# Gated linear attention with a StarReLU layer: from the eighth block on, scaled q and k are transposed by one DMA a block instead of by TensorE

## The chip, the cores and the metric

The kernel runs on one core of a Trainium2 chip. The metric is device time in microseconds (us), from the first to the last instruction of the program on that core; lower is better. The kernel before took 195.38 us (median of 3 runs, 194.61 to 196.4). The engines are called by the profile's names: PE is TensorE's matmuls and PEld its weight loads, DVE is VectorE, ACT is ScalarE, POOL is GpSimd, and SP is SyncE, which in this kernel does nothing but issue DMAs. SPq in a profile row is SP's instruction queue.

## The reference

A recurrence over 768 positions for 4 batches and 8 heads of width 48, and then a two-layer network over the 3072 resulting rows.

```
for t in range(S):
    state = alpha[:, :, t, :, None] * state + einsum('bhd,bhe->bhde', k[:, :, t], v[:, :, t])
    y[:, :, t] = einsum('bhd,bhde->bhe', q[:, :, t], state)
x = y.transpose(0, 2, 1, 3).reshape(B * S, H * D)          # 3072 x 384
h = x @ w_in                                               # 384 -> 2048
r = maximum(h, 0)
out = (s * (r * r) + b) @ w_out                            # 2048 -> 384
```

All inputs and the output are float32; the kernel multiplies in bf16 and adds up in float32.

## The kernel before

The sequence is cut into chunks of 128 positions: 6 chunks a batch, so 24 blocks, numbered n. A block goes through these steps, which are functions of the kernel:

- `load(n)`: four DMAs from SP's queue (L127) bring alpha, k, q and v of the block, 192 KB each, into rings of 8 buffers.
- `ln(n)` takes the logarithm of alpha on ACT (L192), `cum(n)` sums it along the chunk by one matmul into `ct_ps` (L199), and two activations give `bi_sb` = exp(-sum) (L210) and `b_sb` = exp(sum) (L211).
- From block 5 on, where the block is not the last of its batch, `cum` calls `decay(n)`. This takes the last row of `b_sb`, which is the decay over the whole chunk, to a small buffer in memory (`row_dr`, L219) and back into `blast`, with one value a partition (two DMAs, L221). The second step has to wait until the first has landed. All three are issued from SP.
- `vcast(n)` turns v into bf16 on POOL (L195).
- `qk(n)`: two DVE products write scaled k into `kb_sb` (L227) and then scaled q into `qb_sb` (L228), both bf16, with the heads padded from 48 to 64 columns.
- `tr(n)`: eight PE transposes against an identity (L233) write qb and kb, transposed, into PSUM (`t_ps`, the same bank as `ct_ps`), and one DVE copy (L238) takes the 112 x 1024 values into `qkT`.
- `amat(n)`: eight matmuls give k q^T for each head (L248), and two DVE products apply the causal mask (L256, `am_a` and `am_b`).
- `y(n)`: matmuls with the state so far (L267) and with the masked products (L276) give y; L287 gives the chunk's own part of the state, which DVE (L323) and POOL (L328, L332) add and multiply by `blast`.
- `xt(n)` transposes y (L301); `m` does four groups of 12 matmuls of the first layer (L354), with the relu on ACT (L368) and the square on DVE (L375); `o` does 16 matmuls of the second layer (L392), and the result is stored by DMA. The results of the first 14 blocks are kept on the chip and get their bias (L431) and are stored (L428) later, between the other stores, from about position 126 on.

No scheduler moves anything: each step is entered in a list with a position, and the instructions of all engines and queues are issued in the order of the positions. A block is 8 positions long, and block n's `y` stands at p = 8n. The steps ahead of it stand at p - c and so on, where from block 8 on c = 14.8 (`cum`), t = 10.8 (`tr`) and a = 7.9 (`amat`); for blocks 5 to 7 they stand closer to p. `load(n + 4)` stands at p - 2.5. Each engine and each queue works through its own instructions strictly in that order, and an instruction that waits holds everything behind it.

All bulk DMAs, the small ones of `decay` and the stores are issued from SP's queue. The tiles of the pipeline are rings: 2 buffers of `qb_sb`, 3 of `kb_sb`, 2 of `qkT`, 3 of `b_sb` and `blast`.

Of the kernel before, what the change touches and what calls it, by code (L numbers as in the profile page):

```python
# [9 lines left out]
BF16 = mybir.dt.bfloat16  # L10
AF = mybir.ActivationFunctionType
ALU = mybir.AluOpType

@with_exitstack
def kernel(
# [12 lines left out]
    nc = tc.nc  # L28

    B, H, S, D = q.shape  # L30
    C = 128
    NCH = S // C
# [9 lines left out]
    UNITS = 5  # L42
    assert sum(GROUPS) == NBLK
    NLD = 8

    ctx.enter_context(tc.manual_schedule())
    sb = ctx.enter_context(tc.tile_pool(name="sb", bufs=1))
# [16 lines left out]
    def ring(name, shape, dtype, n):  # L64
        return [sb.tile(shape, dtype, name=f"{name}{i}") for i in range(n)]
# [9 lines left out]

    q_sb = ring("q_sb", [128, H, 48], FP32, NLD)
    k_sb = ring("k_sb", [128, H, 48], FP32, NLD)
    v_sb = ring("v_sb", [128, H, 48], FP32, NLD)
    al_sb = ring("al_sb", [128, H, 48], FP32, NLD)
    la_sb = ring("la_sb", [128, H, 64], BF16, 2)  # L80
    b_sb = ring("b_sb", [128, H, 48], FP32, 3)
    bi_sb = ring("bi_sb", [128, H, 48], FP32, 2)
    qb_sb = ring("qb_sb", [128, H, 64], BF16, 2)
    kb_sb = ring("kb_sb", [128, H, 64], BF16, 3)
    v_bf = ring("v_bf", [128, H, 48], BF16, 3)
    y_bf = ring("y_bf", [128, H * 48], BF16, 2)
    qkT_sb = ring("qkT", [128, 2, NP, 128], BF16, 2)
    am_sb = [ring("am_a", [128, NP, 128], BF16, 2), ring("am_b", [128, NP, 128], BF16, 2)]
    blast = ring("blast", [128, NP, 1], FP32, 3)
    row_dr = [dr.tile([1, H * 48], FP32, name=f"row_dr{i}") for i in range(3)]  # L90
# [27 lines left out]
    def src(t, n):  # L118
        b, c = n // NCH, n % NCH
        return t[b, :, c * C : (c + 1) * C, :].rearrange("h s d -> s h d")  # L120

    def load(n, parts=1):
        if n < NBLK:
            for dst, t in ((al_sb, alpha), (k_sb, k), (q_sb, q), (v_sb, v)):
                for i in range(parts):
                    hs = slice(i * H // parts, (i + 1) * H // parts)
                    nc.sync.dma_start(out=dst[n % NLD][:, hs], in_=src(t, n)[:, hs])  # L127

# [62 lines left out]
    def ln(n):  # L191
        nc.scalar.activation(out=la_sb[n % 2][:, :, 0:48], in_=al_sb[n % NLD], func=AF.Ln)  # L192

# [3 lines left out]
    def cum(n):  # L197
        la = la_sb[n % 2]
        nc.tensor.matmul(out=cum_ps, lhsT=U_bf, rhs=la[:, :, 0:48], start=True, stop=True)  # L199
        if n < NCH - 1:  # L200
            for p in range(NP):
                nc.tensor.matmul(  # L202
                    out=tot_ps[0:112, p : p + 1],
                    lhsT=la.rearrange("a h d -> a (h d)")[:, 128 * p : 128 * p + 112],
                    rhs=ones_c,
                    start=True,
                    stop=True,
                )
        cv = cum_ps.rearrange("a (h d) -> a h d", h=H)
        nc.scalar.activation(out=bi_sb[n % 2], in_=cv, func=AF.Exp, scale=-1.0)  # L210
        nc.scalar.activation(out=b_sb[n % 3], in_=cv, func=AF.Exp)  # L211
        if n < NCH - 1:
            nc.scalar.activation(out=blast[n % 3][0:112, :, 0], in_=tot_ps[0:112], func=AF.Exp)
        elif n % NCH < NCH - 1:
            decay(n)

    def decay(n):
        row = row_dr[n % 3]
        nc.sync.dma_start(out=row, in_=b_sb[n % 3].rearrange("s h d -> s (h d)")[127:128])  # L219
        for e in range(2):  # L220
            nc.sync.dma_start(  # L221
                out=blast[n % 3][64 * e : 64 * e + 48, :, 0],
                in_=row.rearrange("o (p e d) -> e d (o p)", e=2, d=48)[e],
            )

    def qk(n):
        nc.vector.tensor_tensor(out=kb_sb[n % 3][:, :, 0:48], in0=k_sb[n % NLD], in1=bi_sb[n % 2], op=ALU.mult)  # L227
        nc.vector.tensor_tensor(out=qb_sb[n % 2][:, :, 0:48], in0=q_sb[n % NLD], in1=b_sb[n % 3], op=ALU.mult)  # L228

    def tr(n):  # L230
        for x, t in ((0, qb_sb[n % 2]), (1, kb_sb[n % 3])):
            for p in range(NP):
                nc.tensor.transpose(  # L233
                    out=t_ps[0:112, x, p, :],
                    in_=t.rearrange("a h d -> a (h d)")[:, 128 * p : 128 * p + 112],
                    identity=ident,
                )
        nc.vector.tensor_copy(  # L238
            out=qkT_sb[n % 2][0:112].rearrange("a x p t -> a (x p t)"),
            in_=t_ps[0:112].rearrange("a x p t -> a (x p t)"),  # L240
        )
# [209 lines left out]
    for t in la_sb:  # L451
        nc.vector.memset(t, 0.0)
    nc.vector.memset(ones_c, 1.0)
    for t in qb_sb + kb_sb + blast:
        nc.vector.memset(t, 0.0)
    make_identity(nc, ident)
    for i in range(NP):
# [8 lines left out]
    def at(pos, fn, *args):  # L466
        events.append((pos, len(events), fn, args))
# [24 lines left out]
    for pos, what in enumerate(  # L492
        [
            (ln, 0), (vcast, 0), (cum, 0), (qk, 0), (spread,), (busy, 3), (tr, 0), (busy, 1), (ln, 1), (vcast, 1), (amat, 0),
            (cum, 1), (busy, 3), (yp, 0), (qk, 1), (st, 0), (busy, 1), (tr, 1), (xt, 0), (busy, 2), (amat, 1),
            (win, 0), (win, 1), (busy, 5), (yp, 1), (ln, 2), (st, 1), (busy, 1), (xt, 1), (cum, 2), (mr, 0, 0), (vcast, 2),
            (qk, 2), (mr, 0, 1), (sq, 0, 0), (mr, 0, 2), (mr, 0, 3), (tr, 2), (sq, 0, 1), (busy, 3), (amat, 2), (sq, 0, 2),
            (win, 2), (busy, 5), (ln, 3), (yp, 2), (st, 2), (cum, 3), (mp, 0, 4), (xt, 2), (rl, 0, 4), (vcast, 3), (qk, 3),
            (mr, 0, 5), (sq, 0, 3), (mr, 1, 0), (sq, 0, 4), (tr, 3), (mr, 1, 1), (sq, 0, 5), (amat, 3), (win, 3), (mr, 1, 2),
            (sq, 1, 0), (busy, 2, y_ps), (yp, 3), (sq, 1, 1), (st, 3), (mr, 0, 6), (xt, 3), (mr, 0, 7), (sq, 1, 2), (sq, 0, 6),  # L500
            (wout, 0), (mr, 1, 3), (sq, 0, 7), (m, 2, 0), (sq, 1, 3), (m, 2, 1), (wout, 1), (o, 0, 0), (m, 2, 2), (o, 1, 0),
            (m, 2, 3), (o, 2, 0), (wout, 2), (o, 0, 1), (o, 1, 1), (colsum, 1), (ln, 4), (wout, 3), (o, 2, 1), (cum, 4), (o, 0, 2), (vcast, 4), (qk, 4), (o, 1, 2), (o, 2, 2), (colsum, 2), (o, 0, 3),
            (o, 1, 3), (tr, 4), (o, 2, 3), (o, 3, 0), (amat, 4),
        ]
    ):
        at(0.1 * pos, *what)
# [12 lines left out]
    for n in range(4, NBLK):  # L519
        p = 8 * n  # L520
        if n > 4:
            f = min((n - 5) / 3.0, 1.0)
            c, t, a = 9.0 + 5.8 * f, 5.8 + 5.0 * f, 3.4 + 4.5 * f
            at(p - c - 1.9, ln, n)
            at(p - c + 0.01, vcast, n)
            at(p - c, cum, n)
            at(p - c + 0.2, qk, n)
            at(p - t, tr, n)
            at(p - a, amat, n)

        e = 0.8 if n == NBLK - 1 else 0.0
        at(p - e, y, n)
        if n + 4 < NBLK:
            at(p - 2.5, load, n + NLD - 4)
        for u in range(4):
            at(p + (2.5, 3.5, 5.5, 7.5)[u], m, group_of[n][0], u)
            at(p + (8.5, 9.5, 12.5, 14.5)[u], o, n, u)
        at(p + 1.0 - e, xt, n)
# [32 lines left out]
```

## Time and profile before

| | |
|---|---|
| median of the runs | 195.38 us (194.61, 195.38, 196.4) |
| span of the profiled execution | 194.6 us |
| granted TensorE clock | 1.000 |
| PE busy | 183.1 us (94%), 2390 matmuls |
| DVE busy | 152.4 us (78%) |
| ACT busy | 119.3 us (61%) |
| POOL busy | 62.1 us (32%) |
| DMA queue of SP | 113550 packets, 29.94 MB, 76.4% of 16 engines' span |

The page gives no time of its own for the profiled execution beside the span of 194.6 us; it lies next to the fastest of the three runs, 0.8 us under their median. Busy time is a share of the whole span, and the stages differ: the first 42 us are the start with the loads of the weights, then follow the blocks at an even pace, and the last 5 us are the tail of the second layer. In every stretch of 14 us between 60 and 186 us PE is busy for 13.88 us or more.

Two kinds of rows are used below. Rows of the timeline give the start, the length, the engine, the line and operation, the tile written and the tiles read, and in brackets how long the engine was idle before and what ended it. Rows of the chain give the start, the length and the work on the chain that ended last. The end of a matmul is modelled, so its cost is read from start to start.

### The profile page before, as it was taken

How to read it: one execution, taken by the hardware profiler on the slowest of the kernel's cores; microseconds unless marked ns; L12 is line 12 of the kernel's file. 1: busy time of each engine (PE TensorE's matmuls, PEld its weight loads, DVE VectorE, ACT ScalarE, POOL GpSimd, SP SyncE). 2: the span in 40 equal slices, each digit the busy share in tenths (PEclk: the TensorE clock that was granted, in tenths of full speed). 3: DMA queues.
4: the chain of work that ended last, by engine and by line, in shares of the span. 5: the costliest groups of instructions: out<-in, count | busy, mean ns of one | idle time of the engine just before them, and what ended most of it. 6: DMA issues, size and time to landing. Idle time of an engine off the chain costs nothing.

```text
span 194.6 us, 6011 instructions
## 1 busy us (share of the span) xinstructions
PE 183.1 (94%) x2390; PEld 144.4 (74%) x2390; DVE 152.4 (78%) x295; ACT 119.3 (61%) x244; POOL 62.1 (32%) x96
## 2 busy tenths in 40 slices
PE   0998978999999999999999999999999999999994
PEld 0566566856777788778878888888877977877783
DVE  5477779965687788888887996878988999998532
ACT  3346395673677666766677576675675666654640
POOL 5143250401300515624500642642501563352000
PEclk9999999999999999999999999999999999999999
DMA  7999889999995856984958458959795965433212
GB/s 124 190 333 176 228 157 369 367 176 198 187 171 90 161 95 93 151 140 79 183 94 163 88 92 152 154 88 192 140 217 148 210 135 115 128 119 121 84 40 81
DMA packets 113581, 30.31 MB, mean 156 GB/s; under 512 B 106755, under 2 KB 112018, under 8 KB 113554
## 3 DMA queue, kind: packets, MB, share of 16 engines
q1 hardware_dynamic: 113550, 29.94, 76.4%
q8 instruction: 18, 0.29, 0.7%
q14 instruction: 9, 0.07, 0.1%
q10 hardware_dynamic: 4, 0.00, 0.0%
HBM read 25.19 MB, written 4.74 MB: 154 GB/s over the span
## 4 chain that ended last, share of the span: by engine, by line
PE 74%; SPq 14%; DMA 6%; ACT 2%; issue 1%; DVE 1%; ACTq 0%
PE o_ps L392 28%; PE h_ps L354 27%; SPq L127 11%; DMA al_sb<-in_alpha_dram 6%; PE ct_ps L233 5%; PE a_ps L248 3%; PE h_ps L301 2%; PE y_ps L276 2%; SPq L136 2%; PE ct_ps L199 2%; PE a_ps L415 1%; PE a_ps L392 1%; PE y_ps L267 1%; SPq L131 1%; PE p_ps L287 1%
## 5 line engine op out<-in xcount | busy, mean ns | idle before, releaser
L368 ACT ACTIVATE r_sb<-h_ps 128x512 bf16<-128x512 f32 x92 | 54.7, 596 | 35.5 <-PE h_ps L354 33.4
L354 PE MATMUL h_ps<-xd_all,w_in_bf 128*128 128x128 bf16 (+1 forms) x1074 | 72.9, 220 | 0.4 <-ACT w_in_bf L143 0.3
L354 PEld LDWEIGHTS <-w_in_bf 128*128 128x128 bf16 x1104 | 68.0, 98 | 7.0 <-issue 0.5
L392 PE MATMUL o_ps<-w_out_bf,gt_all 128*128 128x384 bf16 x336 | 68.3, 326 | 0.1
L375 DVE TENSOR_TENSOR gt_all<-r_sb 128x512 bf16<-128x512 bf16 x96 | 46.8, 503 | 22.2 <-ACT r_sb L368 21.6
L328 POOL TENSOR_TENSOR sd_sb<-t_sb,blast 48x192 bf16<-48x192 f32 x40 | 20.2, 506 | 90.0 <-DVE t_sb L323 54.7
L392 PEld LDWEIGHTS <-gt_all 128*128 128x128 bf16 x368 | 32.6, 98 | 16.1
L195 POOL CAST v_bf<-v_sb 128x384 bf16<-128x384 f32 x24 | 17.0, 710 | 25.1 <-DMA v_sb<-in_v_dram 24.9
L332 POOL TENSOR_TENSOR sc_sb<-t_sb,blast 112x384 f32<-112x384 f32 x16 | 22.6, 1413 | 1.3
L307 ACT ACTIVATE xd_all<-h_ps 128x384 bf16<-128x384 bf16 x24 | 11.8, 490 | 14.3 <-PE h_ps L301 14.3
L238 DVE COPY qkT<-ct_ps 112x1024 bf16<-112x1024 bf16 x24 | 16.4, 682 | 4.9 <-PE ct_ps L233 3.4
L227 DVE TENSOR_TENSOR kb_sb<-k_sb,bi_sb 128x384 bf16<-128x384 f32 x24 | 13.6, 568 | 6.9 <-ACT bi_sb L210 6.8
L256 DVE TENSOR_TENSOR am_a<-a_ps,mask 128x512 bf16<-128x512 f32 x24 | 16.4, 684 | 2.5 <-PE a_ps L248 2.5
L228 DVE TENSOR_TENSOR qb_sb<-q_sb,b_sb 128x384 bf16<-128x384 f32 x24 | 16.4, 683 | 0.9 <-ACT r_sb L368 0.9
L256 DVE TENSOR_TENSOR am_b<-a_ps,mask 128x512 bf16<-128x512 f32 x24 | 16.3, 681 | 0.0
L192 ACT ACTIVATE la_sb<-al_sb 128x384 bf16<-128x384 f32 x24 | 12.4, 517 | 4.1 <-DMA al_sb<-in_alpha_dram 3.9
L210 ACT ACTIVATE bi_sb<-ct_ps 128x384 f32<-128x384 f32 x24 | 11.7, 487 | 4.5 <-PE ct_ps L202 3.5
L199 PE MATMUL ct_ps<-la_sb,U_bf 128*128 128x384 bf16 x24 | 8.1, 340 | 6.1 <-ACT la_sb L192 6.1
L294 ACT ACTIVATE y_bf<-y_ps 128x384 bf16<-128x384 f32 x24 | 11.7, 487 | 1.6 <-PE y_ps L276 1.6
L211 ACT ACTIVATE b_sb<-ct_ps 128x384 f32<-128x384 f32 x24 | 11.8, 493 | 0.0
L233 PEld LDWEIGHTS <-qb_sb 128*112 128x112 bf16 x96 | 8.7, 136 | 3.8 <-DVE qb_sb L228 2.5
L248 PE MATMUL a_ps<-qkT 48*128 48x128 bf16 x192 | 9.8, 222 | 0.8 <-DVE qkT L238 0.7
(67 smaller groups left out, 197.4 us busy)
## 6 DMA issues: line engine op xcount, KB each, us to landing
al_sb<-in_alpha_dram SPq DMA_DIRECT2D x22, 192.0 KB, 3.5
k_sb<-in_k_dram SPq DMA_DIRECT2D x22, 192.0 KB, 4.0
q_sb<-in_q_dram SPq DMA_DIRECT2D x22, 192.0 KB, 4.3
v_sb<-in_v_dram SPq DMA_DIRECT2D x22, 192.0 KB, 4.3
w_in_st<-in_moe_w_in_dram SPq DMA_DIRECT2D x4, 768.0 KB
w_out_st<-in_moe_w_out_dram SPq DMA_DIRECT2D x4, 768.0 KB, 9.7
out_dram<-w_in_st SPq DMA_DIRECT2D x14, 192.0 KB, 2.0
out_dram<-out_sb SPq DMA_DIRECT2D x9, 192.0 KB
```

Of the source, the lines that this page charges most:

```text
L127: nc.sync.dma_start(out=dst[n % NLD][:, hs], in_=src(t, n)[:, hs])
L195: nc.gpsimd.tensor_copy(out=v_bf[n % 3], in_=v_sb[n % NLD])
L228: nc.vector.tensor_tensor(out=qb_sb[n % 2][:, :, 0:48], in0=q_sb[n % NLD], in1=b_sb[n % 3], op=ALU.mult)
L233: nc.tensor.transpose(out=t_ps[0:112, x, p, :], in_=t.rearrange("a h d -> a (h d)")[:, 128 * p : 128 * p + 112], identity=ident,)
L238: nc.vector.tensor_copy(out=qkT_sb[n % 2][0:112].rearrange("a x p t -> a (x p t)"), in_=t_ps[0:112].rearrange("a x p t -> a (x p t)"),)
L256: nc.vector.tensor_tensor(out=am_sb[e][n % 2], in0=a_ps[e], in1=mask4, op=ALU.mult)
L328: nc.gpsimd.tensor_tensor(out=sd[r, :, d], in0=t1_sb[r, :, d], in1=bl[r].to_broadcast([48, NP, 48]), op=ALU.mult)
L332: nc.gpsimd.tensor_tensor(out=sc_sb[0:112], in0=t1_sb[0:112], in1=bl[0:112].to_broadcast([112, NP, 96]), op=ALU.mult)
L354: nc.tensor.matmul(out=hp[:, jj * N : (jj + 1) * N], lhsT=w_in_bf[:, kk, 128 * j : 128 * (j + 1)], rhs=xd_sb[g][:, kk, 0:N], start=(kk == ...
L368: nc.scalar.activation(out=rs, in_=h_of.pop((g, u)), func=AF.Relu)
L375: nc.vector.tensor_tensor(out=gt_sb[g][:, u * 512 : (u + 1) * 512], in0=rs, in1=rs, op=ALU.mult)
L392: nc.tensor.matmul(out=op[:, 0:d_model], lhsT=gt_sb[g][:, j * N + t * C : j * N + (t + 1) * C], rhs=w_out_bf[:, j, :], start=(j == 0), sto ...
```

## The change

Scaled q and k of a block now lie in one tile, `qk_sb` (128 x 2 x 8 x 64, a ring of 3), and `qb_sb` and `kb_sb` are views of it, so `qb_sb` has three buffers and no longer two. From block 7 on (`XBAR = 7`) `tr(n)` issues no PE instruction and no DVE copy: one transposing DMA, from SP's queue, reads the 128 x 1024 bf16 values of `qk_sb` (256 KB) and writes `qkT`. These are 17 of the 24 blocks.

Three steps move. `tr(n)` of these blocks stands 1.4 positions behind `cum(n)`, at p - 13.4, where it stood at p - 10.8. `decay` is split: the row goes out from `cum` as before, and the two DMAs that bring it back stand 0.1 position behind `tr`, for every block that has them. `load(n + 4)` of these blocks stands at p - 5.0 and not p - 2.5. `amat` and all that follows keep their positions.

```diff
-    qb_sb = ring("qb_sb", [128, H, 64], BF16, 2)
-    kb_sb = ring("kb_sb", [128, H, 64], BF16, 3)
+    qk_sb = ring("qk_sb", [128, 2, H, 64], BF16, 3)
+    qb_sb = [t[:, 0] for t in qk_sb]
+    kb_sb = [t[:, 1] for t in qk_sb]
...
         elif n % NCH < NCH - 1:
-            decay(n)
+            nc.sync.dma_start(out=row_dr[n % 3], in_=b_sb[n % 3].rearrange("s h d -> s (h d)")[127:128])
 
     def decay(n):
+        if n < NCH - 1 or n % NCH == NCH - 1:
+            return
         row = row_dr[n % 3]
-        nc.sync.dma_start(out=row, in_=b_sb[n % 3].rearrange("s h d -> s (h d)")[127:128])
         for e in range(2):
             nc.sync.dma_start(
...
     def tr(n):
-        for x, t in ((0, qb_sb[n % 2]), (1, kb_sb[n % 3])):
+        if n >= XBAR:
+            nc.sync.dma_start_transpose(
+                out=qkT_sb[n % 2].rearrange("a x p t -> a (x p) t"),
+                in_=qk_sb[n % 3].rearrange("a x h d -> a (x h d)"),
+            )
+            return
+        for x, t in ((0, qb_sb[n % 3]), (1, kb_sb[n % 3])):
...
             at(p - c + 0.2, qk, n)
+            if n >= XBAR:
+                t = c - 1.4
             at(p - t, tr, n)
+            at(p - t + 0.1, decay, n)
             at(p - a, amat, n)
...
         if n + 4 < NBLK:
-            at(p - 2.5, load, n + NLD - 4)
+            at(p - (5.0 if n >= XBAR else 2.5), load, n + NLD - 4)
```

In the instruction lists of the two kernels, PE loses 17 x 8 transposes with their weight loads, DVE loses 17 copies, and SP's queue gains 17 transposing DMAs. From block 8 on its order within a block is: row, transposing DMA, two DMAs of `blast`, four loads, and then the stores where there are any. Each transposing DMA waits for DVE (the products of `qk`) and for PE (the last reader of that `qkT` buffer, two blocks earlier); the first weight load of `amat` waits for the DMA.

More of the change, by code (lines that the diff above doesn't have):

```diff
@@ L44 @@
     NLD = 8
+    XBAR = 7
     ctx.enter_context(tc.manual_schedule())
@@ L227, in qk @@
         nc.vector.tensor_tensor(out=kb_sb[n % 3][:, :, 0:48], in0=k_sb[n % NLD], in1=bi_sb[n % 2], op=ALU.mult)
-        nc.vector.tensor_tensor(out=qb_sb[n % 2][:, :, 0:48], in0=q_sb[n % NLD], in1=b_sb[n % 3], op=ALU.mult)
+        nc.vector.tensor_tensor(out=qb_sb[n % 3][:, :, 0:48], in0=q_sb[n % NLD], in1=b_sb[n % 3], op=ALU.mult)
     def tr(n):
-        for x, t in ((0, qb_sb[n % 2]), (1, kb_sb[n % 3])):
+        if n >= XBAR:
[5 more added lines that the diff above has]
+        for x, t in ((0, qb_sb[n % 3]), (1, kb_sb[n % 3])):
             for p in range(NP):
@@ L453 @@
     nc.vector.memset(ones_c, 1.0)
-    for t in qb_sb + kb_sb + blast:
+    for t in qk_sb + blast:
         nc.vector.memset(t, 0.0)
```

## The prediction

> **What bounds the kernel now.** I read the chain of waits first. It runs through PE for 74% of the span; before 42 us it is the start's DMAs, which the change leaves alone. One block of it:
>
> ```profile
> 102.70 0.65 PE o_ps L392 x4
> 103.36 0.45 PE ct_ps L233 x8
> 103.80 0.67 PE h_ps L354 x12
> ...
> 106.17 0.33 PE a_ps L248 x8
> 106.50 0.76 PE o_ps L392 x4
> 107.25 0.17 PE h_ps L301 x3
> 107.42 0.16 PE ct_ps L199
> ```
>
> The pieces follow one another without a gap: PE is the bound, and the eight transposes (L233) cost it 0.45 us a block. `amat` (L248) stands 2.8 us behind them, and the next block's `cum` (L199) 1.2 us behind that. Blocks 8 to 23 take PE (171.15 - 65.83)/15 = 7.02 us each, from one start of L199 or L248 to the next.
>
> Second, DVE's timeline in the same stretch, for the slack ahead of `amat`:
>
> ```profile
> 101.97 0.55 DVE L228 TENSOR_TENSOR qb_sb<-q_sb,b_sb 128x384 bf16<-128x384 f32 x1
> ...
> 104.05 0.68 DVE L238 COPY qkT<-ct_ps 112x1024 bf16<-112x1024 bf16 x1
> ```
>
> With `cum` of this block at 100.39, qb is ready at 102.52 (2.13 us later) and `amat` starts at 106.10. So a transposing DMA has 3.6 us, and 3.1 to 3.2 once PE loses its 0.45 us.
>
> Third, SP's timeline, since the new DMA goes into that queue:
>
> ```profile
> 103.43 1.29 SPq L127 DMA_DIRECT2D v_sb<-in_v_dram  x1
> 104.82 0.39 SPq L219 DMA_DIRECT2D row_dr<-b_sb  x1
> 107.21 0.81 SPq L221 DMA_DIRECT2D blast<-row_dr  x2
> 108.07 0.44 SPq L127 DMA_DIRECT2D al_sb<-in_alpha_dram  x1
> 108.60 0.53 SPq L127 DMA_DIRECT2D k_sb<-in_k_dram  x1
> 109.23 1.75 SPq L127 DMA_DIRECT2D q_sb<-in_q_dram  x1
> 111.03 0.94 SPq L127 DMA_DIRECT2D v_sb<-in_v_dram  x1
> 112.06 0.39 SPq L219 DMA_DIRECT2D row_dr<-b_sb  x1
> ```
>
> SP works back to back, with one wait, 2.0 us for the row to land. Row 104.82 belongs to block 13, whose `b_sb` was ready at 101.85: SP is 3 us late. It was 5.5 us late in block 7 (row at 66.33, `b_sb` at 60.8) and 6.1 in block 8, caught up by block 18, and fell 2.6 behind again by block 21. Nothing feels this now, since `blast` is needed only some 12 us after `cum`. In the changed kernel `amat` feels it at once.
>
> **Part by part.** *Removed from PE:* 17 blocks x 0.45 us = 7.65 us, on the path, so -7.65; PE's block becomes 6.57 us. The shared PSUM bank is freed too; PE waits for it nowhere in a full block, so nothing.
>
> *Removed from DVE:* 17 x 0.68 = 11.6 us. DVE is busy 5.2 to 6.9 us of each 7 and is no bound: nothing, save that it keeps up with a shorter block (fullest stretch 6.94 of 7, less 0.68, is 6.3).
>
> *The transposing DMA's latency.* No row of the trace shows one. Its floor is a `blast` DMA, 0.8 KB landing in 1.8 us; its nearest neighbour by source is a 192 KB store, 2.0 us; its ceiling is a load, 192 KB in 3.5 to 4.3 us, which by bytes is 5.7 for 256 KB. I build it from the row DMA right ahead of it: SP sees that land 2.4 to 3.1 us after its issue (104.82 to 107.21, 124.38 to 127.55), because up to two loads are still in the queue. Loads issued back to back pass at one per 1.0 us (41.90 to 53.66), so 256 KB adds 1.4. From 0.45 us after the row this makes 3.3 to 4.1; I take 3.4, near the low end, because a queue that waits for qb has drained further. PE's loop is then: latency L, 1.16 us from `amat` to the next `cum`, 2.13 to qb; so a block takes L + 3.3 = 6.7 us instead of 6.57. Over the nine blocks 8 to 16: +1.1.
>
> The Trainium skill (DMA: Bandwidth & Descriptors, Latency and other measured facts) gives 261 GB/s for a transposing DMA, and its Anatomy section a fixed 2.0 us; my estimate from it is 1.0 + 2.0 = 3.0 us, and the sum by it would lose the +1.1.
>
> *Its time on SP.* Rows go from 0.25 us (a row) to 1.9 (a throttled load). Anything up to some 2 us is hidden in the wait for the row; I take nothing, but where a block has no row (11, 17, 23) it is one more issue of 0.4 to 0.5 us, within SP's reserve there (row 10 to row 12: 11.49 us for two blocks).
>
> *Entering the regime.* Block 6's row goes out at 58.63 as now. Then stand the four loads at 1.0 us each (to 63.0), `blast` (63.9), row 7, and the transposing DMA at 64.4. With L = 3.4 it lands at 67.8; PE would reach `amat(7)` at 65.83 - 0.45 = 65.4. PE waits 2.4, once, and is coupled to SP from there. +2.4.
>
> *The stretch with stores.* SP's rows go out at 137.56, 145.19, 152.97 and 161.10: blocks of 7.63, 7.78 and 8.13 us, since two or three stores join the loads. Only slack hides this now. In the changed kernel row and transpose wait for SP, so PE's three blocks become 23.5 us instead of 19.7: +3.8, less the 0.8 us that SP waited ahead of row 18: +3.0. The lower end is nothing, if SP gets ahead.
>
> *Moved:* `blast` comes behind the transpose, the loads ahead of the stores. POOL needs block 13's `blast` (issued 107.21) at 114.42, so 5 us of cover; loads are four blocks ahead. The transpose's waits hold `blast`, loads and stores behind it on SP; with SP late, qb is ready before SP arrives. Memsets and the third buffer: nothing.
>
> Sum: -7.65 + 1.1 + 2.4 + 3.0 = -1.15 us. The profiled execution would span 193.4, and the median, 0.8 above its span, would be 194.2.
>
> **Rivals.** *A, SP and DMA keep up.* If L stays under 3.25 us and the stores hide, only the entry costs: -7.65 + 1.5 to 2.4, so 189.2 to 190.1. For it: the 192 KB store's 2.0 us; in nine blocks without stores SP needs 6.45 us on average, under PE's 6.57. Against it: SP's lateness throughout.
>
> *B, slower: the transpose is late in every block.* Place: the wait of `amat`'s first weight load. It decides from L = 3.7 us: then L + 3.3 equals today's 7.02, and nothing is won. At the loads' 4.3 us a block takes 7.6: 16 x 0.6 = +9.6, with the entry at 3.3, so 208.3; at L = 4.0, +4.5 and 3.0: 202.9; at the ceiling of 5.7 us, 16 x 2.0 + 4.7: 232. An SP that needs over 2 us to issue it acts the same way, twice: it delays L, and lengthens SP's own block. For it: my build-up of L reaches 4.1. Against it: the row's 3.1 us is at a queue that is full behind a late SP, which a PE that waits lets drain.
>
> On this the Trainium skill speaks against the change: Advanced Engine Details and Errata, DGE: Hardware vs Software, calls the transpose efficiency of hardware descriptor generation, which SP uses, the worse of the two. No row here shows it; it would be rival B.
>
> That the change doesn't take place is no rival: the instruction lists show 136 PE transposes gone.
>
> **The numbers.** A difference under about 1% (1.95 us) can't be told from none. The forecast has 0.5; its own range, with L from 3.25 to 3.6 and the stores from 0 to 3.8, is 190.5 to 197.0, of which 0.24 lies under 193.4, 0.22 within 1% and 0.04 above. Rival A has 0.16, rival B 0.34. So faster 0.40, same 0.22, slower 0.38. The range goes from 189.2 (A's best) into B as far as 207, where about 0.12 of B stays out above; with a little under 189.2, 0.15 is outside.
>
> **What would show it.** Right: PE's chain loses L233 after 62 us; `amat`'s weight load waits for DMA in most blocks, 0.1 to 0.3 us, about 2.4 us in block 7 and about 1 us in blocks 19 to 21; SP's rows 6.6 to 6.8 us apart without stores. Wrong: waits at L248 of more than 0.5 us in every block, or an SP row for the transpose above 2 us (B); none after block 8 (A). If the profile shows `amat` waiting for DVE, or POOL for `blast`, another step has failed.

## The result, and the profile after

| | before | after |
|---|---|---|
| median of 4 runs each | 195.03 us | 213.3 us (211.5 to 215.14) |
| ratio | | 1.0906 (95%: 1.0831 to 1.0981) |
| profiled execution: span, granted clock | 194.6 us, 1.000 | 213.4 us, 0.968 |

The changed kernel is 9% slower. Ratios, here and below, leave out runs more than 1.5% above the fastest of their kernel, the profiled one of 215.14 us among them. In every run on record the time is 1.7 to 1.9 us above the span; so the span of 194.6 us before belongs to the run of 196.4 us, the longest of its kernel and not one near the fastest, and the two profiles compare the longest runs of both. Line numbers move up by up to nine: `amat` is L257 (was L248), `cum` L201, the second layer L401, the first L363, `qk` L230 and L231, the row L217, `blast` L224, the loads L129; the transposing DMA is L235.

From the page of the changed kernel: PE's busy share, the granted clock in 40 slices, SP's DMA queue, and the chain by engine.

```profile
PE 182.1 (85%) x2254; PEld 140.5 (66%) x2254; DVE 140.4 (66%) x276; ACT 119.2 (56%) x244; POOL 52.2 (24%) x96
...
PEclk9999999999999799999999999999996997699999
...
q1 hardware_dynamic: 131502, 34.40, 87.1%
...
PE 56%; DMA 27%; SPq 11%; ACT 2%; issue 2%; DVE 1%; ACTq 0%
```

PE has lost 136 transposes and is busy 85% of a longer span (94% before). DMA has 27% of the chain and had 6%; the DMA into `qkT` alone has 24%. The clock, 1.0 in every slice before, now falls in three places. SP's queue moves 17,952 packets more, 1056 for each transpose. PE's two rows in the table of waits name the place:

```profile
PEld L257 <- DMA qkT<-qk_sb: 22.0, 13, 3.6
PE a_ps L257 <- DMA qkT<-qk_sb: 19.9, 13, 3.3
```

The chain in the stretch that was shown of before (start, length, work):

```profile
101.52 3.11 DMA qkT<-qk_sb
104.63 0.05 issue
104.67 0.40 PE a_ps L257 x8
...
105.99 0.16 PE ct_ps L201
...
106.81 1.22 PE h_ps L363 x22
108.03 4.28 DMA qkT<-qk_sb
112.31 0.05 issue
112.35 0.40 PE a_ps L257 x8
```

Where one PE piece followed the other without a gap, each block now closes the same loop: the transpose lands, `amat`, `cum`, the two products, the next transpose. Two things set a block: the time from the issue of the DMA to `amat` (here 3.15 and 4.32 us, called L as in the prediction), and the time from `amat` to the next issue (here 3.36). SP's timeline in the same stretch:

```profile
107.31 0.25 SPq L217 DMA_DIRECT2D row_dr<-b_sb  x1
108.03 1.24 SPq L235 DMA_TRANSPOSE qkT<-qk_sb  x1
111.56 0.81 SPq L224 DMA_DIRECT2D blast<-row_dr  x2
112.42 0.44 SPq L129 DMA_DIRECT2D al_sb<-in_alpha_dram  x1
112.91 0.57 SPq L129 DMA_DIRECT2D k_sb<-in_k_dram  x1
113.53 0.80 SPq L129 DMA_DIRECT2D q_sb<-in_q_dram  x1
114.37 0.70 SPq L129 DMA_DIRECT2D v_sb<-in_v_dram  x1
115.12 0.90 SPq L217 DMA_DIRECT2D row_dr<-b_sb  x1
116.13 1.24 SPq L235 DMA_TRANSPOSE qkT<-qk_sb  x1
```

Issuing a transpose takes SP 1.24 us, and the wait for the row behind it has grown: 4.25 us from the row's issue to `blast` here, 3.3 on the mean of the 15 rows (2.5 before). The four loads come behind that, and the next transpose (116.13) follows them by one row.

Read from the starts of L248 before, and of L235 and L257 after:

| | `amat` to `amat`, before | forecast | after | of it L | of it `amat` to next issue |
|---|---|---|---|---|---|
| start of `amat` in block 7 | 65.83 | 67.8 | 68.24 | 3.23 | |
| blocks 8 to 17, mean of 9 | 7.08 us | 6.7 | 7.68 | 4.09 | 3.59 |
| blocks 18 to 23, mean of 5 | 7.06 us | 7.8 in three of them | 9.07 | 3.85 | 5.22 |

Over all 17 transposes L falls into two groups: eight from 3.09 to 3.37 us, eight from 4.06 to 5.11, one of 3.59 between. (Where PE comes to `amat` after the landing, L is an upper bound; the 4.06, in block 22, is one of these.)

What sets the groups apart stands in the view of the DMA queues. Beside SP's queue the page has a queue q8 of the kind `instruction`, with 17 transfers of 16 KB (0.28 MB in all), and the kernel before has 18 of them. In the 3.0 us behind the issue of a transpose, such a transfer starts in seven of the 17 blocks: 9, 10, 13, 16, 17, 20 and 21, which are those with an L of 4.12 to 5.11. In the other ten none does, and L is 3.09 to 3.59 there, and 4.06 in block 22.

Three of the waits cost more than their length. Both fences are of the changed kernel: PE's timeline, with the wait in brackets, and windows; in a window row the granted clock stands third from the end, before the DMA share and GB/s.

```profile
160.11 0.40 PE L257 MATMUL a_ps<-qkT 48*128 48x128 bf16 x8 [3.15 <-DMA qkT<-qk_sb]
...
179.36 0.61 PE L257 MATMUL a_ps<-qkT 48*128 48x128 bf16 x8 [3.35 <-DMA qkT<-qk_sb]
```

```profile
157.75:161.16 3.41, 1.05 (x14) 0.69 (x14) 1.02 (x3) 0.00 (x0) 2.28 (x4) 1.00 0.62 100
161.16:164.57 3.41, 3.41 (x25) 2.56 (x24) 1.70 (x4) 1.35 (x4) 0.00 (x0) 0.50 1.11 211
...
180.00:187.00 7.00, 7.00 (x54) 5.11 (x54) 3.63 (x7) 2.56 (x6) 0.00 (x0) 0.64 0.28 65
```

With the waits of 3.20 us (block 7), 3.15 and 3.35 the clock falls to 0.50, for 3.41, 3.41 and 6.83 us (from 69.00, 161.16 and 178.23). In the window from 180 us PE is busy all 7.00 us and does 54 matmuls, where the window from 100 us has 95 in 6.67 us. The mean of 0.968 over the span is worth (1 - 0.968) x 213.4 = 6.8 us.

The account then closes: 7.65 us of transposes gone, 19.9 us of waits at `amat` added, 6.8 us of clock, together +19.05 us; measured are 213.4 - 194.6 = +18.8. By stretch, from `amat` to `amat`, +3.9 us of it lie in blocks 6 to 8, +5.4 in 8 to 17 and +10.1 in 18 to 23; the rest is under half a microsecond each.

### The profile page after: what moved, and what is told of

It is laid out like the page before. It is cut to its first block, busy times and chain, and to the rows that moved or that the text cites. A ratio compares the mean times of both kernels' runs of the same rounds, so it can differ in the third digit from the quotient of the medians.

```text
span 213.4 us, 5728 instructions
## 1 busy us (share of the span) xinstructions
PE 182.1 (85%) x2254; PEld 140.5 (66%) x2254; DVE 140.4 (66%) x276; ACT 119.2 (56%) x244; POOL 52.2 (24%) x96
## 4 chain that ended last, share of the span: by engine, by line
PE 56%; DMA 27%; SPq 11%; ACT 2%; issue 2%; DVE 1%; ACTq 0%
DMA qkT<-qk_sb 24%; PE o_ps L401 22%; PE h_ps L363 21%; SPq L129 10%; PE a_ps L257 4%; DMA w_in_st<-in_moe_w_in_dram 3%; PE a_ps L401 2%; PE h_ps L310 2%; PE ct_ps L201 2%; PE a_ps L424 1%; SPq L133 1%; PE y_ps L285 1%; ACT r_sb L377 1%; PE ct_ps L242 1%; PE y_ps L276 0%
## 5 line engine op out<-in xcount | busy, mean ns | idle before, releaser
L363 PEld LDWEIGHTS <-w_in_bf 128*128 128x128 bf16 x1104 | 71.5, 100 | 9.5 <-issue 1.5
L363 PE MATMUL h_ps<-xd_all,w_in_bf 128*128 128x128 bf16 (+1 forms) x1074 | 75.7, 225 | 0.3 <-ACT w_in_bf L145 0.3
L401 PE MATMUL o_ps<-w_out_bf,gt_all 128*128 128x384 bf16 x336 | 71.0, 336 | 0.0
L384 DVE TENSOR_TENSOR gt_all<-r_sb 128x512 bf16<-128x512 bf16 x96 | 41.9, 446 | 36.0 <-ACT r_sb L377 35.6
L401 PEld LDWEIGHTS <-gt_all 128*128 128x128 bf16 x368 | 33.3, 100 | 17.2 <-issue 1.9
L316 ACT ACTIVATE xd_all<-h_ps 128x384 bf16<-128x384 bf16 x24 | 11.8, 490 | 33.3 <-PE h_ps L310 33.3
L257 PE MATMUL a_ps<-qkT 48*128 48x128 bf16 x192 | 10.0, 226 | 20.6 <-DMA qkT<-qk_sb 19.9
L265 DVE TENSOR_TENSOR am_a<-a_ps,mask 128x512 bf16<-128x512 f32 x24 | 16.5, 689 | 14.8 <-PE a_ps L257 14.8
L230 DVE TENSOR_TENSOR qk_sb<-k_sb,bi_sb 128x384 bf16<-128x384 f32 x24 | 15.0, 627 | 11.9 <-ACT bi_sb L212 11.8
L257 PEld LDWEIGHTS <-qkT 48*128 48x128 bf16 x192 | 5.6, 97 | 25.7 <-DMA qkT<-qk_sb 22.0
L197 POOL CAST v_bf<-v_sb 128x384 bf16<-128x384 f32 x24 | 14.5, 607 | 24.6 <-DMA v_sb<-in_v_dram 24.5
L231 DVE TENSOR_TENSOR qk_sb<-q_sb,b_sb 128x384 bf16<-128x384 f32 x24 | 16.1, 673 | 0.0
L341 POOL TENSOR_TENSOR sc_sb<-t_sb,blast 112x384 f32<-112x384 f32 x16 | 15.3, 958 | 1.3
L201 PE MATMUL ct_ps<-la_sb,U_bf 128*128 128x384 bf16 x24 | 8.6, 356 | 5.5 <-ACT la_sb L194 5.5
L213 ACT ACTIVATE b_sb<-ct_ps 128x384 f32<-128x384 f32 x24 | 11.8, 493 | 0.0
L310 PE MATMUL h_ps<-ident,y_bf 128*128 128x128 bf16 x72 | 8.5, 230 | 0.9 <-ACT y_bf L303 0.8
```

The source lines that it names most:

```text
L197: nc.gpsimd.tensor_copy(out=v_bf[n % 3], in_=v_sb[n % NLD])
L231: nc.vector.tensor_tensor(out=qb_sb[n % 3][:, :, 0:48], in0=q_sb[n % NLD], in1=b_sb[n % 3], op=ALU.mult)
L257: nc.tensor.matmul(out=a_ps[e][:, p, :], lhsT=qkT[r0 : r0 + 48, 1, p, :], rhs=qkT[r0 : r0 + 48, 0, p, :], start=True, stop=True,)
L265: nc.vector.tensor_tensor(out=am_sb[e][n % 2], in0=a_ps[e], in1=mask4, op=ALU.mult)
L341: nc.gpsimd.tensor_tensor(out=sc_sb[0:112], in0=t1_sb[0:112], in1=bl[0:112].to_broadcast([112, NP, 96]), op=ALU.mult)
L363: nc.tensor.matmul(out=hp[:, jj * N : (jj + 1) * N], lhsT=w_in_bf[:, kk, 128 * j : 128 * (j + 1)], rhs=xd_sb[g][:, kk, 0:N], start=(kk == ...
```

## The experiments

The theory behind all of them is that PE waits for a transpose that lands late; what they tell apart is why it is late: traffic, the loads ahead of it, `blast`, the stores, the place of `amat`, or the queue. Each run is compared with the kernel before on the same chip. Of the twelve expectations the theory held in one (moves only) and the named rival in four (amat later; both, no loads; issue earlier from 12; ACT's queue); the other seven times lie between the two. "Transposes beside" and "no loads" were executed twice, the others four to ten times.

| | median us | before | ratio (95%) | span us, clock |
|---|---|---|---|---|
| moves only | 195.47 | 195.51 | 0.9985 (0.9958 to 1.0012) | 194.4, 1.0 |
| transposes beside | 200.02 | 195.51 | 1.0217 (1.0138 to 1.0296) | 197.5, 1.0 |
| no loads | 200.43 | 195.51 | 1.0238 (1.0171 to 1.0304) | 198.8, 1.0 |
| amat later | 208.36 | 195.51 | 1.0612 (1.0539 to 1.0685) | 204.8, 0.983 |
| blast behind the loads | 206.53 | 195.09 | 1.0535 (1.0456 to 1.0615) | 202.8, 0.983 |
| both | 201.05 | 195.09 | 1.0253 (1.0171 to 1.0336) | 197.3, 1.0 |
| both, stores late | 197.42 | 195.09 | 1.0105 (1.0068 to 1.0142) | 195.1, 1.0 |
| both, up to block 16 | 196.43 | 195.09 | 1.0053 (1.0009 to 1.0096) | 194.4, 0.991 |
| both, no loads | 197.04 | 195.24 | 1.0074 (1.0031 to 1.0116) | 194.1, 1.0 |
| issue 2.7 earlier | 196.65 | 195.24 | 1.0040 (0.9995 to 1.0084) | 195.1, 0.991 |
| issue 2.7 earlier, from 12 | 197.1 | 195.24 | 1.0101 (1.0015 to 1.0188) | 193.7, 0.998 |
| ACT's queue | 221.29 | 194.88 | 1.1248 (1.1121 to 1.1375) | 219.8, 0.961 |

### Moves only

PE turns every block; only the other moves of the change are left: the split of `decay`, the earlier loads, the common tile.

```diff
-            if n >= XBAR:
-                t = c - 1.4
             at(p - t, tr, n)
-            at(p - t + 0.1, decay, n)
+            at(p - ((c - 1.4) if n >= XBAR else t) + 0.1, decay, n)
...
-        if n >= XBAR:
+        if n >= NBLK:
             nc.sync.dma_start_transpose(
```

> The moves alone: decay split and its second half placed as in the changed kernel, the loads at p - 5.0, qk in one tile; q and k of all blocks are turned by PE and the DVE copy as before. Theory (the transposing DMA's own traffic and its wait cost the time): within 1% of before, 193.5 to 197. Rival SP (the new order of SP's queue holds something up): 200 or more.

195.47 us against 195.51. The moves cost nothing and bring nothing; the whole loss hangs on the DMA.

### Transposes beside

PE turns every block as in the run above, and the 17 transposing DMAs go out as well, into a spare tile that nothing reads.

```diff
+    def tr_beside(n):
+        nc.sync.dma_start_transpose(
+            out=spare[n % 2].rearrange("a x p t -> a (x p) t"),
+            in_=qk_sb[n % 3].rearrange("a x h d -> a (x h d)"),
+        )
...
+            if n >= XBAR:
+                at(p - c + 1.4, tr_beside, n)
             at(p - t, tr, n)
```

> PE turns q and k of all blocks as before, and the 17 transposing DMAs are issued beside it into a tile that nothing reads. So their traffic and SP time are there, and nobody waits for them. Theory (what costs is the wait of amat in PE's order): 194 to 198, the loads have four blocks of reserve. Rival traffic (the DMA engines are full, whoever waits): 205 or more.

200.02 us lies between the two theories: 4.5 us for the traffic and SP's time, with nobody waiting for a transpose. The first row of the table of waits of this run:

```profile
POOL sd_sb L344 <- DMA blast<-row_dr: 39.7, 7, 8.6
```

and three rows of SP's timeline in it:

```profile
105.79 0.48 SPq L218 DMA_DIRECT2D row_dr<-b_sb  x1
106.37 1.35 SPq L235 DMA_TRANSPOSE spare<-qk_sb  x1
110.58 0.82 SPq L225 DMA_DIRECT2D blast<-row_dr  x2
```

Here too SP waits long for the row (4.8 us from its issue to `blast`; 3.3 on the mean of 15 rows, 2.5 before). The packets of SP's queue take 96.2% of the 16 engines' span, and SP falls so far behind that POOL now waits 39.7 us for `blast`. PE feels it late: up to block 20 its blocks are as long as before, and blocks 21 to 23 (7.48, 9.05 and 9.17 us, where 7.0 to 7.1 were needed) hold its loss; the chain goes there through the late alpha loads, the row, `blast` and POOL. So one part of the loss can come without L: a transpose lengthens SP's own block, which before took 6.45 us.

### No loads

The loads of blocks 11 to 23 are left out, so these blocks compute on what their buffers hold; all else is the changed kernel.

```diff
-        if n + 4 < NBLK:
+        if n < XBAR:
             at(p - (5.0 if n >= XBAR else 2.5), load, n + NLD - 4)
```

> The changed kernel without the loads of blocks 11 to 23, which take the data of earlier blocks that lie in the buffers. Theory (the transposing DMA is late because it stands behind the loads in SP's DMA queue): it lands about 3.1 us after issue in every block, PE waits at amat less than 0.5 us a block, and the time falls to 188 to 193. Rival (the transfer itself takes 4 us or more): waits of 1 us and more stay, 205 or more.

The loss falls from 18.3 us to 4.9, but no gain appears: 200.43 us. PE still waits 11.8 us at L257, and -7.65 + 11.8 = +4.15 us is the difference of the spans (198.8 - 194.6 = 4.2), with the clock at 1.0 throughout. Two reasons are in its timeline. First the rows of DVE, POOL and SP between `amat` (109.44) and the next transpose:

```profile
111.14 0.83 POOL L341 TENSOR_TENSOR sc_sb<-t_sb,blast 112x384 f32<-112x384 f32 x1
111.70 0.68 DVE L230 TENSOR_TENSOR qk_sb<-k_sb,bi_sb 128x384 bf16<-128x384 f32 x1 [0.54 <-ACT bi_sb L212]
111.91 0.83 POOL L197 CAST v_bf<-v_sb 128x384 bf16<-128x384 f32 x1
112.30 0.85 DVE L231 TENSOR_TENSOR qk_sb<-q_sb,b_sb 128x384 bf16<-128x384 f32 x1
113.22 1.23 SPq L235 DMA_TRANSPOSE qkT<-qk_sb  x1
```

The product into q takes 0.85 us where POOL works beside it, against 0.55 in the block that the prediction read, and the issue stands 3.78 us behind `amat`, not 3.3. Over blocks 9 to 17 that part is 3.66 us on the mean (3.35 to 3.39 in five of the nine). Second, L itself: 3.10 to 3.46 us in 14 blocks, and 4.89, 3.98 and 4.39 in blocks 10, 13 and 20, although no load is under way. Windows of half a microsecond of this run, first for the transpose issued at 113.22 (`amat` at 116.37), then for the one at 105.46 (`amat` at 109.44); the last number is GB/s, the one before it the mean busy share of the DMA engines:

```profile
114.00:114.50 0.50, 0.50 (x8) 0.37 (x6) 0.50 (x2) 0.23 (x1) 0.00 (x0) 1.00 0.13 24
114.50:115.00 0.50, 0.50 (x8) 0.37 (x6) 0.47 (x2) 0.45 (x2) 0.00 (x0) 1.00 1.11 215
115.00:115.50 0.50, 0.50 (x13) 0.50 (x11) 0.50 (x2) 0.50 (x2) 0.00 (x0) 1.00 1.16 204
115.50:116.00 0.50, 0.50 (x17) 0.45 (x14) 0.30 (x1) 0.50 (x2) 0.00 (x0) 1.00 0.56 83
```

```profile
106.50:107.00 0.50, 0.50 (x10) 0.44 (x8) 0.50 (x2) 0.06 (x1) 0.00 (x0) 1.00 0.80 162
107.00:107.50 0.50, 0.50 (x6) 0.31 (x4) 0.50 (x1) 0.50 (x1) 0.00 (x0) 1.00 3.08 137
107.50:108.00 0.50, 0.50 (x12) 0.50 (x10) 0.47 (x2) 0.45 (x3) 0.00 (x0) 1.00 0.25 16
108.00:108.50 0.50, 0.50 (x16) 0.45 (x13) 0.00 (x0) 0.50 (x3) 0.00 (x0) 1.00 0.36 72
108.50:109.00 0.50, 0.10 (x3) 0.00 (x0) 0.00 (x0) 0.50 (x2) 0.00 (x0) 1.00 1.05 188
```

In the first, about 1.2 us passes before packets move, then come 1.4 us of moving, at 204 to 215 GB/s in the full half microseconds, and some 0.6 us to the waiting engine. In the second the moving halts for almost a microsecond in the middle. The view of the DMA queues for the 3.0 us behind that issue (105.46 to 108.44) has besides SP's queue, q1:

```profile
q8 instruction: 1, 0.02, 2.2%
q14 instruction: 1, 0.01, 1.3%
```

The same stretch of the first, 113.22 to 116.20, has q1 alone. Of all 17 transposes of this run, blocks 10, 13, 17 and 20 have a 16 KB transfer of q8 there: the three late ones, and one of 3.39 us, whose transfer had ended 1.5 us behind the issue. So L was never under 3.09 us, with or without loads; without an instruction transfer it goes up to 3.59 with loads in the queue and to 3.46 here; and the late landings go with the instruction transfers. No run takes these away, so that they are what holds the transpose up is argued from this agreement and not shown by an edit.

### Amat later, blast behind the loads, both

Three runs, each with one or both of these edits to the changed kernel. With the first, `amat` stands at p - 5.0 in the place of p - 7.9, so that PE has more work to do before it asks for the transpose. With the second, the two `blast` DMAs and with them SP's wait for the row come behind the four loads, which then go out at once, behind the transpose.

```diff
+            if n >= XBAR:
+                a = 5.0
             at(p - a, amat, n)
```

```diff
-            at(p - t + 0.1, decay, n)
+            at(p - t + (0.6 if n >= XBAR else 0.1), decay, n)
```

> The changed kernel with amat of blocks 7 to 23 at p - 5.0 in place of p - 7.9 (p - 6.4 in block 7), so behind the next block's cum: the transposing DMA gets 2.4 us more, and a late one no longer holds up the next block's cum. Theory: PE's waits at L257 all but vanish, the clock stays at 1.0, 188 to 194. Rival traffic (the DMA engines can't carry loads, stores and transposes in 6.6 us a block): 200 or more, the waits come back where stores join.

> The changed kernel with the two blast DMAs behind the four loads, so the loads follow the transposing DMA at once and SP waits for no row in between; amat stays at p - 7.9. Theory queue (a transposing DMA that finds the queue empty lands in 3.1 us, one that finds loads in it in 3.4 to 5): the loads drain before the next one, L falls towards 3.1 to 3.4, and PE's loop (L + 3.7) gives blocks of 6.8 to 7.1 us: 198 to 204. Theory loop alone (SP's order doesn't matter): 210 to 215 as the changed kernel.

> Both: blast behind the loads, and amat of blocks 7 to 23 at p - 5.0. Theory queue: SP's cycle falls under 6.6 us where no stores are, the transpose has 2.4 us more, so PE waits at L257 only at the entry and where stores join: 189 to 196. Theory traffic (loads and transposes fill the DMA engines): a cycle of over 7 us stays, 203 to 209 as with amat later alone.

208.36, 206.53 and 201.05 us: of the loss of 18.3 us the first edit takes back about 5, the second about 7, both about 12. The waits at L257 fall from 19.9 us to 11.8, 13.1 and 6.8. With the second edit alone the late landings (3.59 us and more) go from nine to four behind the first block, 4.70, 4.37, 3.83 and 4.24 in blocks 10, 13, 17 and 20. Three of these are the very blocks that are late without any load, and all four have an instruction transfer in the 3.0 us behind the issue, as had seven of the nine (block 21 has one too, and its L is 3.17). So what became fewer is the meetings with such a transfer; that loads behind the wait for the row made the landings late is not shown. Of the 10.6 us by which this run's span is shorter than the changed kernel's, 3.1 lie in blocks 8 to 17 and 5.7 in blocks 18 to 23, where `amat` to the next issue falls from 5.22 to 4.55 us and the half clock from 10.2 us to 3.4. The half clock appears in the profiles of both single runs, with waits of 3.18 us in the one and of 2.58 and 2.07 in the other, and not in that of the run with both; two other executions of that run show 0.983 and 0.975.

### Both, stores late

The kept results of the first 14 blocks go out from position 148 on, closer together, and no longer from 126.2.

```diff
-        at(126.2 + 4.55 * n, store, n, keep_sb[n])
+        at(148.0 + 2.9 * n, store, n, keep_sb[n])
```

> As the run before, and the stores of the kept blocks begin at position 148 (behind the last load) and follow every 2.9 positions, in place of 126.2 and 4.55. Theory queue: the waits of blocks 17 to 21 go too, 188 to 193. Theory traffic: 200 or more.

197.42 us, 3.6 less than with both edits alone, and the spans differ by 2.2. The waits at L257 fall from 6.8 to 3.7 us. The stretch with the stores was a place of loss of its own.

### Both, up to block 16

Only blocks 7 to 16 are turned by DMA; the stretch with the stores is again PE's.

```diff
-        if n >= XBAR:
+        if XBAR <= n < 17:
             nc.sync.dma_start_transpose(
```

The positions of `tr`, `amat`, `blast` and the loads have the same bound.

> As e5_loads_first, but only blocks 7 to 16 are turned by DMA; 17 to 23 go by PE in the places of before. Theory queue: 10 x 0.45 = 4.5 us less PE work, an entry of about 2.4 us and small waits: 192 to 196. Theory traffic: 198 or more.

196.43 us, 1.0053 of before. Ten transposes are off PE (4.5 us), the waits at L257 are down to 2.3 us, nearly all of it at block 7, and there is no gain. The run after next shows what came up instead.

### Both, no loads

As with both edits, and the loads of blocks 11 to 23 are left out again.

```diff
-        if n + 4 < NBLK:
+        if n < XBAR:
             at(p - (5.0 if n >= XBAR else 2.5), load, n + NLD - 4)
```

> As e5_loads_first (blast behind the loads, amat of blocks 7 to 23 at p - 5.0), without the loads of blocks 11 to 23, whose data is taken from the buffers. Theory (what is left of the loss is the DMA engines shared with loads, and the stretch with stores): 190 to 194, the gain on PE minus the entry. Rival (amat's new place costs PE as much as the transposes did, since nothing stands between y and the transposes of y): 195 to 198, with idle time of PE or its loads ahead of L310 in every block.

197.04 us. Only one wait for the transpose is left, 2.1 us at block 7, and blocks 9 to 14 take 6.76 us, against 6.97 before: 0.2 less, where 0.45 were taken off PE. Its waits show where PE now stands:

```profile
PEld L310 <- ACT y_bf L303: 6.7, 13, 1.5
...
PE o_ps L401 <- DVE out_sb L414: 3.1, 6, 0.8
```

`amat` used to fill PE's time between `y` and the transposes of y (L310), while ACT wrote `y_bf`. At its new place it no longer does: PE's weight loads wait 6.7 us there and its matmuls 2.1, against 1.9 and 0.7 over the whole kernel before, and the wait for `out_sb` is new. DVE and ACT now hold 25% of the chain (3% before). So moving `amat` cures one wait and opens another, and even with the loads gone this layout gains nothing on the kernel before. That bears on the run up to block 16 as well, which waits 6.6 us at the same place.

### Issue earlier, with amat in its place

Instead of asking later, the transpose is issued earlier: all steps from `ln` to `tr` of the blocks in question stand 2.7 positions (some 2.3 us) earlier, `amat` stays at p - 7.9, `qkT` has three buffers, `blast` comes behind the loads, and the stores are late. One run from block 7 on, one from block 12.

```diff
+            if n >= XBAR:
+                c += 2.7
             at(p - c - 1.9, ln, n)
...
-            at(p - t + 0.1, decay, n)
+            at(p - t + (3.3 if n >= XBAR else 0.1), decay, n)
```

> The changed kernel with amat left at p - 7.9, and ln, vcast, cum, qk and the transposing DMA of blocks 7 to 23 2.7 positions earlier (2.3 us); qkT has three buffers; blast behind the loads; the late stores of e6. Theory: the transpose has 5.4 us from the end of qk, enough for all that was seen (3.1 to 5.0), and amat again fills the time between y and xt: PE pays the entry (2 to 3 us) and DVE's waits in the stretch with stores, 190 to 194. Rival traffic: 197 or more.

> As e10_earlier_7, but from block 12 on, where SP is less behind. Theory: 12 x 0.45 = 5.4 us less on PE, an entry of 0 to 1 us: 190 to 193. Rival traffic: 195 or more.

196.65 and 197.1 us. From block 7, four waits at L257 remain (0.80 and 2.52 us at the entry, 0.92 in block 20 and 0.66 in block 21); PE has 74% of the chain again. The account of its profile: -7.65 + 4.9 of waits + (1 - 0.991) x 195.1 = 1.8 of clock gives -1.0, and the span is 0.5 above before, so 1.5 us are not accounted for. The half clock lies here at 26.7 to 30.1 us, ahead of the first transpose, so it is not a cost of the change; from `amat` of block 6 to that of block 23 this execution takes 116.8 us against 118.1. From block 12, blocks 14 to 17 take 6.90 us where they took 7.26, and the profiled execution spans 193.7; but the runs of before on that chip span 192.8 to 195.5, and those of this kernel, from 195.56 to 198.94 us, do not bear out a gain. No version was measured as faster than the kernel before.

### ACT's queue

The changed kernel, with the transposing DMA issued from ACT's queue.

```diff
-            nc.sync.dma_start_transpose(
+            nc.scalar.dma_start_transpose(
```

> The changed kernel with one edit: the transposing DMA is issued from ACT's queue and no longer from SP's, so it stands behind no load, row or store of SP's queue; the loads of SP still use the same 16 DMA engines. In the program's order it stands behind two relus of ACT, ready some 0.5 to 1.5 us later than on SP, and holds ACT for its issue of 1.24 us (ACT is busy 4.9 of each 7 us, so it has the room). Theory (the 4.3 to 5.0 us from issue to landing come from standing behind loads in one queue): the latency falls to 3.1 to 3.4 us in the blocks with loads as in those without, and since SP's row no longer waits with it, the stretch with stores runs below 8 us a block and not at 9.07; median 200 to 207 us. Rival (the engines and the memory are shared, the queue does not matter): latency 4 us and more behind loads as before, and the later issue comes on top; median 213 us or more.

221.29 us: the theory of the queue has fallen. The chain of this run:

```profile
89.30 6.06 DMA qkT<-qk_sb
95.41 0.40 PE a_ps L257 x8
...
105.83 4.86 DMA qkT<-qk_sb
110.74 0.47 PE a_ps L257 x8
...
115.37 4.83 DMA qkT<-qk_sb
```

In a queue of its own, with no load ahead of it, the transpose takes 4.1 to 7.1 us in the eleven blocks where PE waits for it, longer than behind SP's loads. So its place in line is not what delays it. Nor can the instruction transfers be the whole of it here: only three of the eleven have one in the 3.0 us behind the issue. What is left is that loads in flight use the same 16 engines, and that a queue of its own lets more of them run beside it. That last reading is argued and not measured alone. ACT's order costs besides: in the last of these blocks the issue came 0.5 us behind the product (ready at 114.89), after a relu.

## Why the prediction was wrong, point by point

The forecast was 194.2 us; rival B, with 0.34, is what happened, in the place that it named, and past its 208.3 for L = 4.3 and past the range. The sum missed by some 20 us. Of this, blocks 8 to 17 hold 8.8 (9 x (7.68 - 6.7)), blocks 18 to 23 hold 8.5 (45.4 against 23.5 + 2 x 6.7), and most of the rest lies in the entry.

- **PE's 0.45 us a block: right.** 136 transposes are gone, and the account closes with 7.65 us. (The 7.02 us a block of before runs from `amat` of block 7 to `cum` of block 23, two different steps; from `amat` to `amat` it is 7.06.)
- **DVE, the PSUM bank, the moves: right.** The run with the moves alone is level with before, and PE's new waits at `amat` name the DMA. POOL did wait for `blast`, twice at the entry (7.56 and 7.52 us), which the forecast named as the sign of another failed step; behind the start no engine waits for POOL in this profile, so it cost nothing.
- **The entry: right place, too small.** Forecast was a wait of 2.4 us, measured are 3.20: PE came 0.4 us earlier than forecast (65.04) and the issue 0.6 later (65.01). The half clock that followed was not forecast. That `amat` starts 2.4 us later than before (68.24 and 65.83) is a coincidence.
- **"I take 3.4" for L: the step that failed.** The forecast took one L for every block, built from the row and the loads in SP's queue; the mean over blocks 9 to 17 is 4.09. In the four of these nine blocks without an instruction transfer L is 3.16 to 3.59, 3.32 on the mean, so for them 3.4 was a good number. In the other five it is 4.33 to 5.11, 4.70 on the mean. The forecast had no term for the transfers of another queue, though the page of the kernel before lists them. That these transfers are the reason is argued from the agreement, as said above; the loads alone are not, since leaving them out keeps blocks 10, 13 and 20 late. The sum needed 3.25 for rival A; the run without loads shows that even there it was not to be had in every block.
- **The loop's 3.3 us beside L: too small.** It is 3.59 here and 3.66 without loads. It was read from one block in which POOL was idle. Six of the nine blocks keep to 3.35 to 3.50 us; in the other three (3.66 to 4.39) a product takes up to 0.99 us in the place of 0.55, and POOL works beside it in the block of the run without loads that is shown above. With the forecast's own L this alone makes 7.0 us a block, which is the kernel before; with both, 7.68.
- **"I take nothing" for SP's issue: mis-sized.** The issue itself is 1.24 us in most blocks (up to 2.58) and lies in the wait for the row. What was left out is that it lengthens that wait: SP's block, row to row from block 7 to 16, is 7.2 us in the run with `amat` later and 7.6 with the transposes beside, where it was 6.45. With no one waiting for the transposes this cost 4.5 us in the second run.
- **The stretch with stores: right place, wrong size.** Forecast were 7.8 us a block for three blocks; measured are 9.07 over five. SP's rows there go out 8.5 to 9.1 us apart (156.37, 164.86, 173.99, 183.00), since the transposes join the stores in the queue, and `amat` to the next issue has grown to 5.22 us.
- **The clock: left out.** In the kernel before, behind 14 us, no stretch of 3.41 us has PE idle for more than 1.0 us, and the clock stays at 1.0. In the changed kernel 6.8 of the 18.8 us are its, 5.1 of them in the stretch with stores.

On the clock the Trainium skill (TensorE: Matmul & The Clock Gate, Why this matters for your kernels) says that gaps of more than about 3 us between bursts of matmuls throw TensorE back to half speed. The trace agrees for the three waits of 3.15 to 3.35 us. The runs put the edge lower and less sharp: 2.07 and 2.58 us were enough in the run with `blast` behind the loads, while 2.93 us (no loads, block 7) left the clock at 1.0. The clock records of the traces bring these together. In each trace the changes of the clock lie whole multiples of 3.41 us apart. Cut the profiles that have such changes, between 60 and 190 us, into stretches on that grid: at a clock of 1.0, each of the ten stretches in which PE is idle for 1.88 us or more is followed by the half clock, and none with 1.75 us or less is. The wait of 2.07 us lies whole in one stretch (151.67 to 155.09), and that of 2.93 us is split over two, in which PE is idle for 1.35 and 1.75 us. In the start and the tail, outside these bounds, two stretches do not fit (1.68 us, then half; 1.97 us, then full).

The Trainium skill's figure from DMA: Bandwidth & Descriptors, which made an estimate of 3.0 us for L, is met by the quickest transposes (3.09 us) and not by the mean; its fixed 2.0 us stands there for DMAs issued through GpSimd, and these are issued from SP. With it the forecast would have been further off still.

## What to carry to other kernels

A transfer that takes the place of engine work is not free because the queue has slack: cost it as a loop, issue to landing and landing to next issue, with the durations of a crowded block, and ask what it does to every other wait on that queue. Look at all queues of the page, also those that the kernel does not issue to. Give it more lead than its slowest landing, here 5 us and not 3.4, or leave the work on the engine that does it in 0.45 us. And where PE is the bound, price a wait of 2 to 3 us at its length and again at the half clock that may follow, here 1.7 us for each 3.41 us of it.

## What the runs showed of the hardware

- A transposing DMA of 256 KB within the chip's own buffers: 1.24 us of issue on SP, 1.25 on ACT, 3.1 us from issue to the waiting engine at best, 204 to 215 GB/s in full half microseconds while it moves. On ACT's queue, where its packets are counted apart (17,956 packets, 14.8% of 16 engines' 219.8 us), one takes 29 ns on the mean; those of SP's queue take 21 (113,550 packets, 68.5%); both means mix packet sizes and crowded stretches. The rule named in the prediction from the Trainium skill (Advanced Engine Details and Errata, DGE: Hardware vs Software) compares hardware descriptor generation with software's; no run here has a transpose by software's, so none tests it.
- It comes 0.7 to 2 us later than that in some blocks, and in blocks 10, 13 and 20 so in the changed kernel, with `blast` behind the loads, and with no loads at all. In these three runs a 16 KB transfer of the kind `instruction` starts within 3.0 us behind the issue of 16 of the 51 transposes, and L is 3.8 us or more in 14 of these (3.17 and 3.39 in the others); of the 35 without, all are at 3.60 or less but the 4.06 where PE came late. How such a transfer holds a transpose up was not measured.
- The granted clock falls to 0.50 for 3.41 us or twice that, on a grid of 3.41 us, behind stretches of that grid in which PE was idle for 1.88 us and more, as told above.
- Issuing only k or only q by DMA, and so halving each transfer, was not tried.
